# A branch for few tokens in the first half of the first layer, in three blocks of the last group

## The chip, the cores and the metric

One core of one Trainium2 chip. The metric is the device time of one execution in microseconds, as the median of several runs.

## What is computed

Linear attention with positive random features, then a layer of eight experts of which each token takes one. The attention output (4608 tokens of 512 values) is the experts' input; `e_idx` routes each token by the largest of its eight gate logits.

```python
for e in range(E):
    mask = e_idx == e
    h = np.maximum(x[mask] @ w1[e], 0.0)      # 512 -> 1024
    ye = h @ w2[e]                            # 1024 -> 512
    out[mask] = gate_w[mask, None] * eom[mask, e, None] * ye
```

## The kernel before, in words

The attention part works through 32 units and leaves its rows in DRAM. While it runs, tokens are routed in four groups; each group is cut into blocks of 128 tokens of one expert each. A block is one call of `item(n)` (line 1474 on). Blocks 0 to 24 belong to the first three groups. The last group holds blocks 25 to 48; in the part of the program that always runs (up to the first tail branch) these are blocks 25 to 37, thirteen of them. Blocks 25 to 35 are sure to hold tokens; 36 and 37 stand under a test of a flag (line 1491). With the data at hand the tail after them is not entered.

The work of a block on TensorE (PE) is cut in halves, which the text calls first half and second half of the first layer, and first and second half of the second layer:

- the first layer, `hidden(g, w_)` (line 1580), g = 0 and 1: 48 matmuls each (line 1588), a weight quarter of 128 x 128 as the stationary side and `w_` token columns as the moving side. Weights stand in fp16 as a high and a low part (`w1h`, `w1l`);
- `relu` on ScalarE (ACT, line 1595) and `rest` on VectorE (DVE, line 1599) make the high and low parts of the hidden values, `hh` and `hl`;
- the second layer, `second(g, w_)` (line 1604): 12 matmuls of 512 columns per half (line 1619), or 24 of 256 columns for few tokens (line 1611);
- `scaled` on ACT and `put` on GpSimd (POOL) write the rows out.

In the last group a block's second half of the first layer and its first half of the second layer are one step, "hB" (`hidden_and_second`, line 1626). The steps of neighbouring blocks alternate: the first half of block n's first layer ("hA"), the second half of block n-1's second layer ("out"), then block n's "hB".

A block with at most 64 tokens is one with few tokens. Its flag `few` is computed on the chip, loaded into a register of each engine (`load_flags`, line 1382), and tested by `either` (line 1567; the branch is line 1573 in the profile), which writes a step's code twice, for 64 and for 128 columns:

```python
with tc.If(regs[n, "few", (eng,)] > 0) as small_block:
    fn(FEW)
with small_block.Else():
    fn(P)
```

Before, in the last group all steps of a block but one go through `either`; the first half of the first layer does not and always takes 128 columns.

When the next block has another expert, its weights are brought in by SyncE (`bring`, lines 1507 and 1509; tiles `r`, `es`, `xs` and others), and cut into high and low parts by ACT (`high`, line 431) and DVE (`low`, line 435), a quarter at a time, as soon as the block before no longer needs that quarter. The last group has such changes of expert at blocks 26, 31 and 37.

The order of all steps is a table written out by hand (`ORDER`), and so are the PSUM banks; each engine's instructions stand in the program in that order. The code of all blocks is unrolled; there is no loop.

Of the kernel before, what the change touches and what calls it, by code (L numbers as in the profile page):

```python
# [21 lines left out]
P = 128  # L22
# [32 lines left out]
EARLIER = (8, 8, 9)  # L55
# [5 lines left out]
KS = (*EARLIER, NITEM - ISSUED[-1])  # L61
# [3 lines left out]
TAIL = (13, 18)  # L65
# [261 lines left out]
def attention_moe(ctx: ExitStack, tc: tile.TileContext, kqt, kqn, v, om, wg, w1, w2, cf, cm, ci, out):  # L327
# [1049 lines left out]
    slots = [(g, i) for g in range(NG) for i in range(KS[g])]  # L1377
    regs = {}
    EVERY = ("PE", "DVE", "ACT", "POOL", "SP")
    ENGINES = {"PE": ENG.PE, "DVE": ENG.DVE, "ACT": ENG.Activation, "POOL": ENG.Pool, "SP": ENG.SP}  # L1380

    def load_flags(n0, n1, row, engs):
        g, i = slots[n0]
        src = tabs[g]["few"][:, 0] if row == "few" else tabs[g]["ctl"][:, row]
        _, got = nc.values_load_multi_w_load_instructions(
            src[0:1, i : i + n1 - n0], engines=[ENGINES[e] for e in engs]
        )
        for m in range(n0, n1):
            regs[m, row, engs] = got[m - n0]
# [22 lines left out]
    def flags(g):  # L1412

        base = sum(KS[:g])
        R = -1000.0 + g
        sets = ("PE",), ("DVE",), ("ACT",), ("POOL",), ("SP",)
        cuts = sorted({base, base + KS[g], *(n for n in tail if base < n < base + KS[g])})

        def load(n0, n1, row, engs, part):
            after = [("limits" if row == "few" else "controls", g)] + ([("gi", g)] if g < NG - 1 else [])  # L1420
            if n0 >= 4:
                after.append(("out", n0 - 4, 1))
            plan.part = part
            plan.add(
                ("flag", n0, row, engs), engs, 0.5, lambda: load_flags(n0, n1, row, engs), after=after, rank=R,
            )
            plan.part = 0
            for m in range(n0, n1):
                flag_step[m, row, engs] = ("flag", n0, row, engs)

        rows = [(0, base + SURE[g], sets if g == NG - 1 else ()), (1, base, (("SP",), ("ACT", "DVE")) if g < FINE else (("SP",), ("ACT",), ("DVE",)))]
        if g == NG - 1 and FEW:
            rows.append(("few", base, (("PE",), ("ACT",), ("DVE",), ("POOL",))))
        for row, first, sets in rows:
            for a, b in zip(cuts, cuts[1:]):
                if row == 0 and a in tail:
                    load(a, a + 1, 0, EVERY, part_of(a) - 1)
                for n0 in range(max(a, first), b, BATCH):
                    for engs in sets:
                        load(n0, min(n0 + BATCH, b), row, engs, part_of(n0))  # L1440
# [8 lines left out]
    def cuts_of(n, w, parts=range(NQ)):  # L1449

        return [("sw", n, w)] if slots[n][0] < FINE else [("swl", n, w, i) for i in parts]
# [22 lines left out]
    def item(n):  # L1474
# [5 lines left out]
        def add(key, eng, cost, fn, after=(), **kw):  # L1480
            after = list(after)
            if not sure(n):
                after.append(flag_step[n, 0, (eng,)])
            if gr == NG - 1 and FEW and key[0] in ("hA", "hB", "relu", "rest", "out", "os", "put"):
                after.append(flag_step[n, "few", (eng,)])

            def step():
                if sure(n):
                    fn()
                else:  # L1490
                    with tc.If(regs[n, 0, (eng,)] > 0):  # L1491
                        fn()

            plan.add(key, (eng,), cost, step, after=after, **{"rank": R, **kw})
# [72 lines left out]
        def either(eng, fn):  # L1567

            if gr < NG - 1 or not FEW:
                return lambda: fn(P)  # L1570

            def step():
# [5 lines that stand above are left out]
            return step  # L1578

        def hidden(g, w_):  # L1580
            ph = banks["ph", n, g]
            for f4 in range(FC // 2):
                f = g * (FC // 2) + f4
                qd, fo = f // 2, (f % 2) * P
                a = 0
                for kk in range(KC):
                    for w, x in ((w1h, 2 * kk), (w1h, 2 * kk + 1), (w1l, 2 * kk)):
                        nc.tensor.matmul(  # L1588
                            ph[:, f4, 0:w_], w[qd][:, kk, fo : fo + P], xt(n)[:, x, 0:w_], start=(a == 0), stop=(a == 3 * KC - 1)
                        )  # L1590
                        a += 1

        def relu(g, w_):
            sl = slice(g * (FC // 2), (g + 1) * (FC // 2))
            nc.scalar.activation(hh(n)[:, sl, 0:w_], banks["ph", n, g][:, :, 0:w_], AF.Relu)  # L1595

        def rest(g, w_):
            sl = slice(g * (FC // 2), (g + 1) * (FC // 2))
            nc.vector.scalar_tensor_tensor(  # L1599
                out=hl(n)[:, sl, 0:w_], in0=banks["ph", n, g][:, :, 0:w_], scalar=0.0, in1=hh(n)[:, sl, 0:w_],  # L1600
                op0=ALU.max, op1=ALU.subtract,
            )
# [27 lines left out]
        for g in range(2):  # L1630
            name = "hA" if g == 0 else "hB"
            both = joint and g
            add(
                (name, n), "PE", 5.2 if both else 2.6,
                either("PE", hidden_and_second if both else lambda w_, g=g: hidden(g, w_)) if g else lambda: hidden(0, P),
                tiles=[("xt", n), ("hh", n), ("hl", n)] if both else [("xt", n)],
                bank=[("b", ("ph", n, g), [FC // 2, P])] + ([("b", ("po", n), [DM])] if both else []),
                after=[("xt", n), *cuts_of(n, 1, halves_of[g])]
                + ([("hA", n)] if g else [("hB", n - 1)] if joint and slots[n - 1][0] == gr else [])
                + ([("rest", n, 0), *cuts_of(n, 2, halves_of[0])] if both else []),  # L1640
                **(dict(early=2.6, lead={("rest", n, 0): 2.6, **{c: 2.6 for c in cuts_of(n, 2, halves_of[0])}}) if both else {}),
            )
            add(
                ("relu", n, g), "ACT", 0.48, either("ACT", lambda w_, g=g: relu(g, w_)), after=[(name, n)], rank=-600.0 + n,
                tiles=[("hh", n)],
            )
            add(
                ("rest", n, g), "DVE", 0.6, either("DVE", lambda w_, g=g: rest(g, w_)), after=[("relu", n, g)], rank=-600.0 + n,
                tiles=[("hh", n), ("hl", n)], frees=[("ph", n, g)],
            )  # L1650
# [43 lines left out]
    for n in range(len(slots)):  # L1694
        item(n)
# [80 lines left out]
```

## Time and profile before

| | |
|---|---|
| median of 3 runs | 621.66 us (620.2 to 622.68) |
| profiled execution, its own time | 623.94 us |
| its span, first to last instruction | 622.1 us |
| TensorE busy | 593.0 us, 95% |
| weight loads of TensorE busy | 470.7 us, 76% |
| VectorE, ScalarE, GpSimd busy | 388.7, 421.4, 373.9 us |
| mean DMA rate | 207 GB/s |

How to read it: a start is in us from the first instruction of the span. A busy time is the union of an engine's instructions, and matmuls overlap in it, so the spacing of their starts tells the rate and not their length. In a timeline row the bracket gives the time the engine stood still before the row and what the profile holds to have ended it; "issue" is a stop for which it shows no wait. "PEldq" is TensorE's sequencer, which reads the program ahead of the matmuls; branches stand there. "SPq" rows are transfers that SyncE issues. The queue "q8 instruction" moves TensorE's program code; its packets are told from the other engines' by their size.

### The profile page before, as it was taken

The page shows a single profiled execution, that of the slowest core. Times are in us where ns is not written, and L with a number is a line of the kernel's source. Part 1 is how long each engine was busy: PE and PEld are TensorE (multiplying, and loading weights), DVE is VectorE, ACT ScalarE, POOL GpSimd, SP SyncE. Part 2 cuts the span into 40 slices and gives each one's busy share as a digit, 9 for nine tenths or more (in the row PEclk, how much of TensorE's full clock was granted, in tenths as well). Part 3 has the DMA queues.
Part 4 walks back from the last instruction along what each step waited for, and adds up shares of the span by engine and source line. Part 5 has one row for each costly group of instructions (what it writes and reads, how often), then busy time and mean ns, then how long its engine had stood idle before and what let it go on. Part 6 is the DMA issues. An engine that isn't in the chain of part 4 may idle for free. (4 is left out here: it accounts for less than half of the span.)

```text
span 622.1 us, 22237 instructions
## 1 busy us (share of the span) xinstructions
PE 593.0 (95%) x8716; PEld 470.7 (76%) x8716; DVE 388.7 (62%) x1219; ACT 421.4 (68%) x978; POOL 373.9 (60%) x275
## 2 busy tenths in 40 slices
PE   6999986999999899999999999999999999999986
PEld 6999875877786677778877777777867867677764
DVE  4877699876688987657797855643783520361125
ACT  6999999789888688889968787872521521351134
POOL 1265589798977688999788789984413121211201
PEclk9999998899999999999999999999999999999999
DMA  7655689999999999999988999768677955842561
GB/s 255 210 167 164 204 286 198 227 224 272 312 259 232 238 255 206 285 199 239 303 217 246 237 204 191 180 168 228 200 155 225 222 102 180 241 79 55 162 224 45
DMA packets 145888, 129.00 MB, mean 207 GB/s; under 512 B 104270, under 2 KB 127440, under 8 KB 144464
## 3 DMA queue, kind: packets, MB, share of 16 engines
q1 hardware_dynamic: 139760, 107.45, 69.4%
q0 software_dynamic: 5984, 19.72, 10.5%
q8 instruction: 80, 1.31, 0.9%
q14 instruction: 64, 0.52, 0.3%
HBM read 83.86 MB, written 19.30 MB: 166 GB/s over the span
## 5 line engine op out<-in xcount | busy, mean ns | idle before, releaser
L1588 PE MATMUL ph<-xt,w1h 128*128 128x128 f16 (+1 forms) x2432 | 206.8, 218 | 3.7 <-issue 1.8
L1588 PE MATMUL ph<-xt,w1l 128*128 128x128 f16 (+1 forms) x1216 | 203.2, 218 | 0.0
L1588 PEld LDWEIGHTS <-w1h 128*128 128x128 f16 x2432 | 184.1, 98 | 12.1 <-issue 3.4
L625 ACT ACTIVATE ef<-pp,nb 128x128 f32<-128x128 f32 x576 | 163.2, 395 | 18.3 <-DVE nb L619 13.9
L606 DVE TENSOR_REDUCE pp<-pp 128x3 f32<-128x384 f32 x192 | 102.9, 558 | 32.8 <-PE pp L584 27.6
L648 POOL TENSOR_TENSOR es<-ef,es 128x1152 f16<-128x1152 f32 x44 | 104.5, 2386 | 25.6 <-ACT es L646 14.9
L1588 PEld LDWEIGHTS <-w1l 128*128 128x128 f16 x1216 | 118.5, 98 | 0.0
L1599 DVE SCALAR_TENSOR_TENSOR hl<-ph,hh 128x512 f16<-128x512 f32 (+1 forms) x76 | 50.5, 665 | 101.0 <-ACTq L1517 64.2
L1619 PE MATMUL po<-w2h,hl 128*128 128x512 f16 x280 | 106.1, 379 | 1.8 <-DVE hl L1599 1.8
L1619 PE MATMUL po<-w2h,hh 128*128 128x512 f16 x280 | 106.2, 379 | 0.2 <-PE ph L1588 0.2
L1619 PE MATMUL po<-w2l,hh 128*128 128x512 f16 x280 | 106.1, 379 | 0.0
L1595 ACT ACTIVATE hh<-ph 128x512 f16<-128x512 f32 (+1 forms) x76 | 44.6, 590 | 89.3 <-PE ph L1588 74.1
L1551 POOL DMA_INDIRECT gx<-rows,gi x38 | 38.8, 1020 | 89.0 <-ACT os L1674 34.7
L1619 PEld LDWEIGHTS <-hh 128*128 128x128 f16 x560 | 51.3, 98 | 52.7 <-issue 0.3
L518 POOL TENSOR_TENSOR xlo<-xt,xhi 128x1152 f16<-128x1152 f32 x24 | 57.1, 2379 | 9.3 <-ACT xhi L511 8.4
L1619 PEld LDWEIGHTS <-hl 128*128 128x128 f16 x280 | 27.4, 98 | 35.3 <-DVE hl L1599 2.3
L1674 ACT ACTIVATE os<-po,gx 128x512 f32<-128x512 f32 (+1 forms) x34 | 23.4, 687 | 43.1 <-PE po L1619 39.5
L646 ACT CAST es<-ef 128x1152 f16<-128x1152 f32 x44 | 51.5, 1181 | 0.7 <-ACTq L1512 0.2
L804 PE MATMUL pn<-kvs,et 128*128 128x81 f16 (+1 forms) x960 | 47.2, 203 | 0.9 <-DVE pp L606 0.5
L804 PEld LDWEIGHTS <-et 128*128 128x128 f16 (+1 forms) x960 | 40.3, 100 | 7.5 <-issue 0.5
L584 PE MATMUL pp<-omh,xhi 64*128 64x128 f16 x432 | 42.3, 222 | 2.7 <-DVE xf L817 0.8
L839 POOL TENSOR_TENSOR xs<-xf,xs 128x576 f16<-128x576 f32 x32 | 41.0, 1282 | 1.1
(193 smaller groups left out, 1057.7 us busy)
## 6 DMA issues: line engine op xcount, KB each, us to landing
r<-w SPq DMA_DIRECT2D x10, 2048.0 KB, 9.5
xt<-kqt SPq DMA_DIRECT2D x32, 576.0 KB, 5.1
xn<-kqn SPq DMA_DIRECT2D x24, 576.0 KB, 5.8
rawv<-v SPq DMA_DIRECT2D x32, 325.0 KB, 4.6
rows<-xs SPq DMA_DIRECT2D x16, 576.0 KB, 5.8
r<-w SPq DMA_DIRECT2D x8, 512.0 KB, 5.9
ef<-w SPq DMA_DIRECT2D x2, 512.0 KB, 4.3
et<-w SPq DMA_DIRECT2D x2, 512.0 KB, 8.1
```

The lines of the kernel that those rows point to most:

```text
L518: lambda t0=t0, t1=t1: nc.gpsimd.tensor_tensor(out=xl(u)[:, t0:t1], in0=xt32(u)[:, t0:t1], in1=xh(u)[:, t0:t1], op=ALU.subtract),
L584: nc.tensor.matmul(banks["pp", 2 * u + i, g][:, c, :], x[r, t], w[r, :], start=(a == 0), stop=(a == len(ops) - 1))
L606: nc.vector.tensor_reduce(out=pp[:, 3, 0:3], in_=pp[:, 0:3, :], op=ALU.min, axis=AX.X)
L625: nc.scalar.activation(ef(n)[:, c, :], banks["pp", n, g][:, c % 3, :], AF.Exp, bias=nb(n)[:, c : c + 1], scale=-SK)
L646: nc.scalar.copy(es(slot_es(n))[:, 0], ef(n))
L648: nc.gpsimd.tensor_tensor(out=es(slot_es(n))[:, 1], in0=ef(n), in1=es(slot_es(n))[:, 0], op=ALU.subtract)
L804: nc.tensor.matmul(pn[lo:hi, c - c0, :], a[:, c, lo:hi], w[:, :, b], start=(i == 0), stop=(i == len(ops) - 1))
L839: nc.gpsimd.tensor_tensor(out=x[:, :, P + o : P + o + D], in0=xf(u)[:, :, 0:D], in1=x[:, :, o : o + D], op=ALU.subtract)
L1588: nc.tensor.matmul(ph[:, f4, 0:w_], w[qd][:, kk, fo : fo + P], xt(n)[:, x, 0:w_], start=(a == 0), stop=(a == 3 * KC - 1))
L1595: nc.scalar.activation(hh(n)[:, sl, 0:w_], banks["ph", n, g][:, :, 0:w_], AF.Relu)
L1599: nc.vector.scalar_tensor_tensor(out=hl(n)[:, sl, 0:w_], in0=banks["ph", n, g][:, :, 0:w_], scalar=0.0, in1=hh(n)[:, sl, 0:w_], op0=ALU.ma ...
L1619: nc.tensor.matmul(po, x(n)[:, f, :], w[f // 2][:, f % 2, :], start=(f == 0 and a == 0), stop=(f == FC - 1 and a == 2))
```

## The change

`either` now also wraps the first half of the first layer, in blocks 25, 36 and 37. `tail_at` is 38, the last group has 24 slots, so `NARROW` is (25, 36, 37).

```diff
+    tail_at = sum(EARLIER) + TAIL[0]
+    NARROW = (len(slots) - KS[-1], tail_at - 2, tail_at - 1)
...
             add(
                 (name, n), "PE", 5.2 if both else 2.6,
-                either("PE", hidden_and_second if both else lambda w_, g=g: hidden(g, w_)) if g else lambda: hidden(0, P),
+                either("PE", hidden_and_second if both else lambda w_, g=g: hidden(g, w_)) if g or n in NARROW else lambda: hidden(0, P),
```

On TensorE, at the start of block 25's first half (`ph_25_0` is its PSUM tile, `xt25` its tokens, `po_24` the second layer of block 24), the program before has:

```order
L1619 LDWEIGHTS hl24_11711
L1619 MATMUL po_24_11772<-w2h1_100,hl24_11711 128x512
L1588 LDWEIGHTS w1h0_91
L1588 MATMUL ph_25_0_11785<-xt25_11749,w1h0_91 128x128
L1588 LDWEIGHTS w1h0_91
```

and now, at the start of the half and at the end of its first copy:

```order
L1622 MATMUL po_24_11772<-w2h1_100,hl24_11711 128x512
L1576 COMPARE_AND_BRANCH
L1591 LDWEIGHTS w1h0_91
L1591 MATMUL ph_25_0_11785<-xt25_11749,w1h0_91 128x64
...
L1591 MATMUL ph_25_0_11785<-xt25_11749,w1l1_96 128x64
L1576 UNCONDITIONAL_BRANCH
L1591 LDWEIGHTS w1h0_91
L1591 MATMUL ph_25_0_11785<-xt25_11749,w1h0_91 128x128
```

The half stands there twice: 48 weight loads and matmuls of 64 columns, a jump, and the 48 of 128 columns as before. Nothing changed places; the program after it stands 98 instructions further on.

The same at the start of block 36's first half on TensorE, now, behind the flag's own test:

```order
L1388 TENSOR_LOAD ctl3_11160
L1494 COMPARE_AND_BRANCH
L1576 COMPARE_AND_BRANCH
L1591 LDWEIGHTS w1h0_91
L1591 MATMUL ph_36_0_15283<-xt36_14953,w1h0_91 128x64
```

Before, the weight load of the 128-column half followed the first of the two branches. Block 37 is like block 36. The other engines' programs have the same instructions in the same order.

## Rows read from the trace of the kernel before

**Rows 1.** The core's span and clock; the page's queue of TensorE's code (packets, MB, share)
```profile
core 0: 622.1 us, clock 0.990
...
q8 instruction: 80, 1.31, 0.9%
```

**Rows 2.** Groups by line and shape, 64-column matmuls: count | busy us, mean ns | idle us
```profile
L1588 PE MATMUL ph<-xt,w1h 128*128 128x64 f16 x96 | 4.6, 193 | 0.0
L1588 PE MATMUL ph<-xt,w1l 128*128 128x64 f16 x48 | 4.5, 193 | 0.0
```

**Rows 3.** Timeline of TensorE, blocks 25 and 26: start us, length us, line, tiles, shape
```profile
482.69 0.27 PE L1588 MATMUL ph<-xt,w1h 128*128 128x128 f16 x2
...
485.37 0.38 PE L1619 MATMUL po<-w2h,hh 128*128 128x512 f16 x1
...
487.96 0.22 PE L1588 MATMUL ph<-xt,w1h 128*128 128x64 f16 x2
...
489.45 0.30 PE L1611 MATMUL po<-w2h,hh 128*64 128x256 f16 x2
...
498.57 0.38 PE L1619 MATMUL po<-w2h,hh 128*128 128x512 f16 x1
```

**Rows 4.** Timeline of TensorE: block 29's first and second half, block 36's second
```profile
522.24 0.28 PE L1588 MATMUL ph<-xt,w1h 128*128 128x128 f16 x2
...
527.51 0.27 PE L1588 MATMUL ph<-xt,w1h 128*128 128x128 f16 x2
...
603.63 0.22 PE L1588 MATMUL ph<-xt,w1h 128*128 128x64 f16 x2
```

**Rows 5.** Timeline of TensorE, the stops from block 25 to block 36
```profile
495.88 0.28 PE L1588 MATMUL ph<-xt,w1h 128*128 128x128 f16 x2 [0.71 <-ACT w2h L431]
...
530.55 0.38 PE L1619 MATMUL po<-w2h,hh 128*128 128x512 f16 x1 [0.20 <-PE ph L1588]
...
594.09 0.29 PE L1588 MATMUL ph<-xt,w1h 128*128 128x128 f16 x2 [1.82 <-issue]
```

**Rows 6.** Line 1573's branches on TensorE's sequencer: ns min/median/max, first and last start us
```profile
L1573 PEldq COMPARE_BRANCH  x1: 86/86/86, 485.1 to 485.1; - x1
...
L1573 PEldq COMPARE_BRANCH  x2: 190/941/1692, 493.8 to 494.1; - x2
...
L1573 PEldq COMPARE_BRANCH  x1: 330/330/330, 587.5 to 587.5; - x1
```

**Rows 7.** DMA queues, windows 493.3:591.8, 496.85:497.0, 535.43:535.6, 591.70:592.0, 598.33:598.5
```profile
q8 instruction: 17, 0.28, 1.2%
...
q8 instruction: 1, 0.02, 44.1%
...
q8 instruction: 1, 0.02, 40.5%
...
q8 instruction: 1, 0.02, 19.9%
...
q8 instruction: 1, 0.02, 42.4%
```

**Rows 8.** Timeline of SyncE: weight loads issued for blocks 26, 31, 37
```profile
483.72 1.77 SPq L1507 DMA_DIRECT2D es<-w  x2
...
522.29 7.89 SPq L1509 DMA_DIRECT2D r<-w  x2
...
586.50 0.36 SPq L1509 DMA_DIRECT2D r<-w  x1
...
592.06 0.36 SPq L1509 DMA_DIRECT2D r<-w  x1
```

**Rows 9.** Timelines of ScalarE, VectorE and TensorE, block 37's weights and last matmuls
```profile
606.70 2.00 ACT L431 ACTIVATE w1h<-r 128x1024 f16<-128x1024 f32 x2 [0.22 <-PE po L1611]
...
607.79 2.36 DVE L435 SCALAR_TENSOR_TENSOR w1l<-r,w1h 128x1024 f16<-128x1024 f32 x2 [0.85 <-ACT w1h L431]
...
616.02 0.30 PE L1611 MATMUL po<-w2l,hh 128*64 128x256 f16 x2 [0.74 <-DVE w2l L435]
```

## Prediction

> **What bounds the kernel.** From the page I took that TensorE is busy nearly all the time; the view of the core gives a mean granted clock of 0.990, so its speed is not in question [rows 1]. Then the groups by shape: first-layer matmuls of 64 columns come 96 and 48 times, three halves of 48 [rows 2]. The timeline shows what a half is worth by the spacing of its starts. Block 25, the last group's first, starts its first half at 482.69 and the next work at 485.37: 48 matmuls in 2.68 us, 0.0558 each. Its second half, with 64 columns, starts at 487.96 and the second layer at 489.45: 0.029 each and a short gap [rows 3]. A second such half starts at 603.63, in block 36 [rows 4]; the third is the last half of all, in block 37. So the three blocks that get a branch are the three that can use it.
>
> Next the idle time of TensorE from block 25 on. It stands still three times before the last block: 0.71 us before 495.88, 0.20 before 530.55, 1.82 before 594.09 [rows 5]. The last falls inside 48 like matmuls and is put down to "issue": the next instruction was not there. The first is put down to a weight cut of ScalarE, but TensorE's own branch into that half, at 494.1, took 1.692 us, to 495.8 [rows 6]; I take it for the same thing. Another branch, at 587.5, took 0.330 [rows 6].
>
> The DMA view has a queue of kind "instruction", 80 packets of 16 KB [rows 1]. From the first of these stops to the last it has 17 [rows 7], and in the built program 16 x 256 instructions lie between the two places. So TensorE's code comes in pieces of 256 instructions, and I can say where their edges are. I count from block 25's first weight load (a matmul is two, a branch one, a branch to the next row none): the last stop comes at position 4673, the others fit, and the edges are at 65 + 256k.
>
> When does a piece come? The edge at 4417 is passed by the branch at 587.5, so at 587.9; the next packet starts at 591.7, and the stop at its end, 594.09, shows that code is usable 2.4 us after its packet starts [rows 5 to 7]. A weight load issued at 586.50 was under way [rows 8]. Likewise 594.1 to 598.33, with the load of 592.06, and 530.6 to 535.43, with the second load of the row at 522.29: 3.8 to 4.8 us from edge to packet [rows 5, 7, 8]. In a quieter stretch it was 1.1, from 495.8 to 496.9 [rows 6, 7]. So a piece needs about 3.4 us in quiet and 6.2 to 7.2 under a load, and only one is asked for ahead. The branch at 485.1 ran when some 42 of 48 matmuls had started: TensorE's queue is read about 36 instructions ahead [rows 3, 6].
>
> **The change, part by part.** Nothing is removed and no step is moved. Each of the three first halves gets a branch, a 64-column copy of 96 instructions and a jump over the old one: 98 more in the program each. The order of steps is a fixed table, so no other engine's work moves.
>
> (a) The matmuls: 48 x (0.0558 - 0.029) = 1.27 us less in each of three blocks, 3.8 in all. The branch costs nothing: it is read while the queue holds second-layer matmuls, as at 485.1, where it took 0.086 us [rows 6]. Without that cover it would be its 0.09, and 0.33 for the jump.
>
> (b) Block 37's share comes to nothing. From 607.79 VectorE splits weights and residues with hardly a gap, and the last second-layer matmuls wait 0.74 for it at 616.02 [rows 9]. That chain starts with ScalarE's cut at 606.70, behind block 36's second half [rows 9], not behind block 37's first. A shorter first half makes TensorE wait longer. Bounds: 0 to 0.7 us won.
>
> (c) Block 25. More code is passed in less time. The edge at 321 is passed at 487.6, in the load issued from 483.72 [rows 8]. With 4.0 us to the packet and 2.4 to its use the piece is there at 494.0. TensorE needs it at position 577, now five matmuls before the end of block 26's first half, at 492.0. It waits 2.0, does 0.3 and 1.4 us more, and starts block 26's second half at 495.7 (before: 495.88). The edge at 833 comes 15 matmuls in; that piece takes 3.3 from 494.0, so 0.8 more is waited. The half ends at 499.1 against 498.57 [rows 3]: 0.5 us lost in place of 1.27 won. Bounds: -2.0 (the 1.27 and the old 0.71, no new wait) to +1.4 (4.8 us to the packet).
>
> (d) Blocks 29 and 30. Their code is the same, 98 places later. The edge at 1857 now lies inside block 29's first half, which starts at 522.24 [rows 4]; it is passed at 522.9, just after the load issued at 522.29 [rows 8]. The edge at 2113 is now the first instruction of block 29's second half, needed at 527.51 [rows 4]; before, it lay past that half and cost the 0.20 at 530.55. With 4.0 + 2.4 the piece is there at 529.3: 1.8 waited. TensorE jumps the edge at 2369 at about 537.1; the piece behind it takes 6.4, to 543.5, and TensorE is at 2625, inside block 30's second half, at 542.4: 1.1 more. Less the 0.2, +2.7 us. Bounds: 0 (the request slips in ahead of the load) to +3.4 (4.8 us).
>
> (e) Blocks 35 and 36, in the times of before. The edge at 4673 is now jumped by the branch into block 35's second half, its piece asked for before the load of 586.50: the stop of 1.82 goes, 2.0 by the matmuls' spacing. Block 36's first half is 1.27 shorter. But the edge at 4929 now lies in it, passed at 596.9 in the load of 592.06, and the edge at 5185 comes 26 matmuls into its second half, 4.3 us later; the piece takes 6.4. New wait 2.1, sum -1.2. Bounds: -3.3 (no new wait) to -0.4 (4.8 us).
>
> (f) In block 37 a piece comes every 3.3 us and TensorE will stop again for a microsecond or two in all; the chain of (b) covers it, and without that cover it would be paid.
>
> Sum: 0.5 + 2.7 - 1.2 = **+2.0 us**. The profiled execution has a span of 622.1 [rows 1] and a time of 623.94; the median of the runs is 621.66. So 624.1 by the span, **623.6** by the median. A measurement of this kernel can tell 0.5%, 3.1 us, from no change: I forecast no change that can be told, to the slow side.
>
> The rows show code waited for while a load is under way [rows 5, 7, 8]. The Trainium skill, page "Runtime: NRT & Kernel Launch", section "Instruction fetch mechanics", says that code streams in 16 KiB blocks of 256 instructions, that crossing an edge is "mostly hidden", and that a taken branch out of the two blocks held stalls. The trace agrees on the block and the branch; it differs on "mostly hidden" inside loads. By that phrase the sum would be (a) without (b), -2.5 us.
>
> **Rivals.** First, the code comes in time: blocks 25 and 36 give 1.27 each, block 37 nothing. For it: only three stops in 110 us. Against it: the same pieces are used up faster, and each edge named above falls into a load. It gives 621.66 - 2.5 = 619.1, and 616.4 if the old stops of (c) and (e) go as well.
>
> Second, slower: every request in a load waits as long as that of 530.6, 4.8 us. Place: edges 321, 1857 and 4929. For it: this is the only request that met the first packets of a load, as 1857's will. Price: 1.4 + 3.4 - 0.4 = 4.4, so 626.1; it passes 3.1 from about 4.4 us on.
>
> Third: the flags choose the full copy and nothing is saved. The 64-column rows, chosen by the same flag, speak against it [rows 2]. The code still moves, so (d) would stay: 624.4.
>
> **How the numbers follow.** Forecast, 0.62: 623.6, own range 620.5 to 625.5, a tenth of it over 624.8. First rival, 0.21, something over half of it under 618.5, where the old stops go too. Second, 0.15, and third, 0.02, over 624.8 for the most part. So faster 0.13, same 0.64, slower 0.23. One case in ten is left out at each end: 618.4, inside the first rival, to 626.1, the second's price.
>
> **What would show it.** In the changed profile the 64-column matmuls double, from 144 to 288. TensorE stops near 492 inside block 26's first half, near 528 before block 29's second, near 542 inside block 30's second and near 604 inside block 36's second; it does not stop inside block 35's second half. Each stop ends about 2.4 us after an instruction packet starts. The last second-layer matmuls still wait for VectorE. I am wrong if TensorE runs through blocks 26 and 29 without a stop (first rival), if a stop there is over 2.5 us (second), or if the end no longer hangs on VectorE.

## The result, and the profile after

The changed kernel takes 625.84 us (median of 16 runs, 622.99 to 631.2), the kernel before, in turn with it on the same chip, 622.17 (16 runs, 619.99 to 628.45). The ratio is 1.0064, with a 95% interval of 1.0042 to 1.0086: **slower by 4.0 us**, 2.6 to 5.4. I had forecast 2.0 more and no change that can be told. The time fell inside my range (to 626.1), at its upper end.

The profiled execution has a span of 622.8 us, hardly more than before [rows 1], but block 25 begins at 480.23 in it and began at 482.69 before. What lies ahead of block 25 differs from run to run by several us (480 to 492 in the seventeen traces of this case), in kernels that are alike there. So the two traces are compared from the start of block 25 to the start of the last matmul: 133.80 us before (482.69 to 616.49), **136.88** after (480.23 to 617.11), 3.1 more. The last matmul is the second of the two in these rows, before and after:

```profile
616.46 0.30 PE L1611 MATMUL po<-w2h,hl 128*64 128x256 f16 x2
```

```profile
617.08 0.30 PE L1614 MATMUL po<-w2h,hl 128*64 128x256 f16 x2
```

The page's queue of TensorE's code, and the groups by line and shape:

```profile
q8 instruction: 81, 1.33, 0.9%
```

```profile
L1591 PE MATMUL ph<-xt,w1h 128*128 128x64 f16 x192 | 9.4, 193 | 2.7 <-issue 2.4 <-PE po L1614 0.3
L1591 PE MATMUL ph<-xt,w1l 128*128 128x64 f16 x96 | 9.2, 193 | 0.0
```

The 64-column matmuls have doubled, from 144 [rows 2] to 288, and those of line 1591 (1588 before) now stand idle for "issue". The timeline of TensorE, blocks 25 and 26, to hold against [rows 3, 5]:

```profile
480.23 0.22 PE L1591 MATMUL ph<-xt,w1h 128*128 128x64 f16 x2
...
481.63 0.38 PE L1622 MATMUL po<-w2h,hh 128*128 128x512 f16 x1
...
487.14 0.28 PE L1591 MATMUL ph<-xt,w1h 128*128 128x128 f16 x2
...
492.70 0.28 PE L1591 MATMUL ph<-xt,w1h 128*128 128x128 f16 x2 [2.87 <-issue]
...
496.79 0.26 PE L1591 MATMUL ph<-xt,w1l 128*128 128x128 f16 x1 [0.46 <-issue]
...
499.00 0.38 PE L1622 MATMUL po<-w2h,hh 128*128 128x512 f16 x1
```

Block 25's first half takes 1.40 us, 481.63 less 480.23, in place of 2.68. Three matmuls before the end of block 26's first half TensorE stops for 2.87. The same stretch in windows (the columns are busy us and count of PE, PEld, DVE, ACT, POOL, then granted clock, DMA share, GB/s):

```profile
489.80:492.70 2.90, 0.03 (x2) 0.01 (x1) 2.33 (x3) 0.79 (x1) 0.00 (x0) 1.00 1.42 261
492.70:494.07 1.37, 1.37 (x23) 1.27 (x25) 0.00 (x0) 0.94 (x2) 0.00 (x0) 1.00 0.52 115
494.07:497.48 3.41, 2.95 (x29) 2.40 (x26) 2.78 (x3) 1.55 (x2) 0.00 (x0) 0.50 0.73 82
497.48:499.00 1.52, 1.52 (x30) 1.52 (x28) 0.18 (x1) 0.00 (x0) 0.00 (x0) 1.00 0.04 11
```

From 494.07, 1.37 us after the stop ended, TensorE's granted clock is 0.50 for 3.41 us, the 1.2 GHz level: 29 matmuls start in that time, where the 1.52 us behind it hold 30. No row of the kernel before had shown this in this stretch. It does not cost what it slows down, because a second stop for code, 0.46 before 496.79, lies inside these 3.41 us: what TensorE did slowly ahead of 496.79 it would else have spent waiting for that piece. The comparison with e6 below puts the price of the low clock at 0.6 us at most.

The later stops, from the same timeline:

```profile
528.30 0.29 PE L1591 MATMUL ph<-xt,w1h 128*128 128x128 f16 x2 [0.19 <-PE po L1622]
...
541.76 0.23 PE L1591 MATMUL ph<-xt,w1h 128*128 128x128 f16 x1 [0.68 <-issue]
...
604.32 0.23 PE L1591 MATMUL ph<-xt,w1h 128*128 128x64 f16 x2 [1.67 <-issue]
...
608.62 0.30 PE L1614 MATMUL po<-w2l,hh 128*64 128x256 f16 x2 [0.67 <-issue]
...
611.98 0.22 PE L1591 MATMUL ph<-xt,w1h 128*128 128x64 f16 x2 [0.68 <-issue]
...
616.64 0.30 PE L1614 MATMUL po<-w2l,hh 128*64 128x256 f16 x2 [0.34 <-DVE w2l L435]
```

The first three are where the forecast put them: ahead of block 29's second half, inside block 30's and block 36's second halves. Those at 608.62 and 611.98 belong to block 36's second layer and block 37, part (f). The stop of 1.82 inside block 35's second half [rows 5] is gone. By stretch, counted from block 25's start:

| up to | before | after | difference in the stretch | forecast |
|---|---|---|---|---|
| end of block 26's second half | 15.88 | 18.77 | (c) +2.89 | +0.5 |
| start of block 31 | 63.57 | 67.34 | (d) +0.88 | +2.7 |
| end of block 36's second half | 122.44 | 124.81 | (e) -1.40 | -1.2 |
| start of the last matmul | 133.80 | 136.88 | (f) +0.71 | 0 |

### The profile page after: what moved, and what is told of

Its sections match the earlier page's. It is cut to its first block, busy times and chain, and to the rows that moved or that the text cites. A ratio compares the mean times of both kernels' runs of the same rounds, so it can differ in the third digit from the quotient of the medians.

```text
span 622.8 us, 22241 instructions
## 1 busy us (share of the span) xinstructions
PE 588.7 (95%) x8716; PEld 466.4 (75%) x8716; DVE 388.6 (62%) x1219; ACT 421.2 (68%) x978; POOL 374.1 (60%) x275
## 5 line engine op out<-in xcount | busy, mean ns | idle before, releaser
L1591 PE MATMUL ph<-xt,w1h 128*128 128x128 f16 (+1 forms) x2432 | 204.7, 218 | 6.6 <-issue 5.9
L1591 PE MATMUL ph<-xt,w1l 128*128 128x128 f16 (+1 forms) x1216 | 200.7, 217 | 0.5 <-issue 0.5
L1591 PEld LDWEIGHTS <-w1h 128*128 128x128 f16 x2432 | 181.8, 98 | 16.4 <-issue 9.3
```

Source lines behind the costliest of these rows:

```text
L1591: nc.tensor.matmul(ph[:, f4, 0:w_], w[qd][:, kk, fo : fo + P], xt(n)[:, x, 0:w_], start=(a == 0), stop=(a == 3 * KC - 1))
```

## The experiments

The theory: TensorE's code comes in pieces, an edge that is passed while a weight load is under way waits for it, and the 98 new instructions in a block move all later edges. The rivals: the branches cost a time of their own; the narrow halves bring nothing; the loss has to do with something else than code. Ratios are against the kernel before, run in turn on the same chip; the groups e1 to e4, e5 to e8, e9 to e12 and e13 to e15 ran on four different chips, on which the kernel before takes 630.6, 630.8, 623.6 and 631.5 us. "Length" is that from block 25's start to the last matmul's start, in the one profiled execution.

| run | ratio, 95% interval | length, us |
|---|---|---|
| changed kernel | 1.0064, 1.0042 to 1.0086 | 136.88 |
| e1, block 25 alone | 1.0010, 0.9982 to 1.0039 | 140.16 |
| e2, blocks 36 and 37 | 0.9991, 0.9962 to 1.0019 | 135.81 |
| e3, gain without code | 0.9949, 0.9917 to 0.9980 | 133.03 |
| e4, code without gain | 1.0019, 0.9992 to 1.0045 | 136.69 |
| e5, kernel before again | 1.0009, 0.9975 to 1.0043 | 136.10 |
| e6, changed kernel again | 1.0031, 1.0001 to 1.0060 | 135.47 |
| e7, no copies | 0.9902, 0.9869 to 0.9935 | 128.52 |
| e8, half loads | 0.9969, 0.9938 to 1.0000 | 132.16 |
| e9, 96 idle instructions | 0.9945, 0.9914 to 0.9975 | 132.04 |
| e10, all thirteen blocks | 1.0129, 1.0085 to 1.0174 | 139.84 |
| e11, copies in three blocks | 0.9990, 0.9963 to 1.0017 | 130.21 |
| e12, the same without the change | 0.9952, 0.9917 to 0.9987 | 130.68 |
| e13, no load for block 26 | 0.9990, 0.9953 to 1.0028 | 132.12 |
| e14, e2 and 48 idle instructions | 0.9961, 0.9928 to 0.9994 | 133.65 |
| e15, e9 again | 0.9982, 0.9956 to 1.0009 | 133.91 |

### Parts of the change: e1 to e4

e1 and e2 take a part of the tuple:

```diff
-    NARROW = (len(slots) - KS[-1], tail_at - 2, tail_at - 1)
+    NARROW = (len(slots) - KS[-1],)              # e1
+    NARROW = (tail_at - 2, tail_at - 1)          # e2
```

> Only block 25 gets the branch and the narrow copy; blocks 36 and 37 are as before. Theory (TensorE's code comes late): block 25's 98 new instructions alone move every later edge, so the stops of 2.9 us in block 26's first half and the small ones in blocks 29 and 30 stay, the old stop of 1.8 us inside block 35's second half goes, and nothing is saved in block 36: +2.9 to the end of block 26's second half, +0.9 more to block 31, -1.9 at block 35, together +2.0 us against the kernel before (ratio about 1.003). Rival (each branch and its jump cost about 1 us where they stand): a third of the whole loss of 3.7 us, +1.2, with 64-column halves followed by a gap at the branch itself and no stop in block 26. Rival (something ahead of block 25 differs): nothing later than block 25 changes in length.

> Blocks 36 and 37 get the branch and the narrow copy; block 25 is as before. Theory (code late): up to block 35 the trace is that of the kernel before (stops of 0.7 in block 26, 0.2 in block 29, 1.8 in block 35). In block 36 1.27 us are saved, and a new stop of about 0.9 comes behind its first half, where the edge that the new code brings is passed in the second weight load: -0.3 us, which is the same time; block 37's share is covered by VectorE's splits. Rival (each branch costs about 1 us): +2.5 us. Rival (code in time, the forecast's first): -1.3 us.

e3 has the narrow halves without branch or second copy, e4 the branch and two copies of 128 columns:

```diff
-either("PE", ... lambda w_, g=g: hidden(g, w_)) if g or n in NARROW else lambda: hidden(0, P)
+... if g else (lambda: hidden(0, FEW)) if n in NARROW else lambda: hidden(0, P)             # e3
+either("PE", ... lambda w_, g=g: hidden(g, w_ if g else P)) if g or n in NARROW else ...    # e4
```

> The first halves of blocks 25, 36 and 37 are done with 64 columns always, without a branch and without the copy of 128 columns (left out: the tokens past 64 that such a block could hold with other data). The matmuls are those of the changed kernel, and the code lies where it lay before the change. Theory (code late): 1.27 saved in block 25, of which the stop in block 26 gives some back (0.7 becomes about 1.6, since the same piece is asked for and wanted earlier); -0.7 to block 35, whose stop of 1.8 stays; -1.27 in block 36, block 37's covered: -2.0 us (bounds -1.3 and -2.6). Rival (the narrow first halves themselves bring nothing, since others wait): 0 or more, and with the changed kernel's loss in them about +3.7.

> The changed kernel with 128 columns in both copies of the three first halves: the same 98 instructions in each place, nothing saved. Theory (code late): stops in blocks 25 and 26, 29, 30 and 36 as in the changed kernel, a little shorter where TensorE now arrives 1.27 us later: about +4 us against the kernel before, within 1 us of the changed kernel, because what is saved there is spent waiting for code. Rival (the loss comes of the 64-column form, the code costs nothing): 0 us. Rival (the change's saving of 2.5 us is real and paid in full): the changed kernel's +3.7 and 2.5 more, +6.2.

e3 decides the first point: the narrow halves alone win 3.2 us (1.3 to 5.2 by the interval). So the matmuls that the change saves are worth what they seemed (the 2.0 expected lies inside the interval), and the new code costs more than they give. The stop of 1.6 that I expected in e3's block 26 did not come; the 1.81 in block 35 stayed. e4, the code alone, comes out at +1.2 us (-0.5 to +2.8): less than the 4 expected, which lies outside the interval; 0, the first rival's value, lies inside. Its trace has the "issue" stops of block 26's second half (1.43), block 30 (0.23) and block 36 (0.45), shorter than the changed kernel's. e1 and e2 are both the kernel before's time within their intervals; they do not tell the parts apart. In e1's trace the stop is in block 26's second half, 4.46 us long, and the clock falls behind it as in the changed kernel:

```profile
504.98:508.39 3.41, 3.41 (x30) 2.86 (x28) 0.02 (x1) 0.60 (x1) 0.00 (x0) 0.50 0.42 75
```

e1's length is the longest of all and its time is not, so single traces of block 26 differ more than I had thought.

### The two kernels again, all copies gone, and lighter loads: e5 to e8

e5 and e6 are the two kernels unchanged.

> The kernel before once more, for a trace from the chip of the runs beside it. Theory (code late): the stops that hang on the place of the code come again at the same instructions, at the 18th matmul of block 35's second half (1.7 to 2.1 us) and ahead of block 29's second-layer work (0.2 to 0.5); their length may differ by a microsecond, since it hangs on when the weight load begins. If the 1.85 us that the runs without a change in blocks 36 and 37 also waited in block 36's second-layer work, behind ScalarE, come here too, they belong to the chip and not to an edit. Rival: the stops move about from run to run.

> The changed kernel once more, beside the kernel before on the same chip. Theory (code late): stops at the same instructions as before: in block 26 at the 45th matmul of the first half or the 14th of the second, 1.6 to 4.6 us together; ahead of block 29's second half; at the 37th matmul of block 30's second half; at the 27th of block 36's second half. From block 25's start to the last matmul it is 2 to 4 us longer than the kernel before, and the ratio of the times lies between 1.003 and 1.007. Rival (the loss comes from another part of the program): the distance from block 25's start to the last matmul is the same in both.

The stops came at the same instructions. In e5 TensorE stands 1.84 us behind the 18th matmul of block 35's second half, and 0.75 ahead of block 29's second layer (0.2 to 0.5 expected); in e6 there are stops behind the 45th matmul of block 26's first half and the 14th of its second, ahead of block 29's second half, behind the 37th matmul of block 30's second half and the 27th of block 36's, as in the first trace. But block 26's are 0.52 and 1.16 here, and no clock falls behind them:

```profile
500.86 0.29 PE L1591 MATMUL ph<-xt,w1h 128*128 128x128 f16 x2 [0.52 <-issue]
...
504.68 0.22 PE L1591 MATMUL ph<-xt,w1l 128*128 128x128 f16 x1 [1.16 <-issue]
...
506.57 0.38 PE L1622 MATMUL po<-w2h,hh 128*128 128x512 f16 x1
```

From the first stop's end to the second's, and from there to the end of the half, in windows, first e6, then the changed kernel's first trace:

```profile
500.86:504.68 3.82, 2.66 (x42) 2.24 (x42) 3.14 (x6) 2.49 (x3) 0.00 (x0) 1.00 0.53 77
504.68:506.57 1.89, 1.89 (x34) 1.89 (x34) 1.15 (x2) 0.00 (x0) 0.00 (x0) 1.00 0.04 9
```

```profile
492.70:496.79 4.09, 3.63 (x41) 2.98 (x42) 2.09 (x3) 2.49 (x3) 0.00 (x0) 0.67 0.75 103
496.79:499.00 2.21, 2.21 (x34) 2.21 (x34) 0.87 (x1) 0.00 (x0) 0.00 (x0) 0.84 0.09 14
```

Ahead of the second stop TensorE is busy 3.63 us for the same work that takes it 2.66 in e6, and yet this stretch is only 0.27 longer: the piece comes when it comes. Behind it the low clock costs 0.32 more. So by this comparison at most 0.6 of the two stretches' 6.30 us are the clock's.

Block 26's load starts at another moment against the code, first in the changed kernel's first trace, then in e6:

```profile
481.25 1.97 SPq L1510 DMA_DIRECT2D es<-w  x2
```

```profile
487.24 0.93 SPq L1510 DMA_DIRECT2D es<-w  x2
```

That is 1.0 us behind block 25's start at 480.23, and 2.8 us ahead of block 25's start at 490.04. In e6 another request met it, the one behind the edge at 65: its packet comes 3.9 us behind block 25's start (493.98), where it came 1.6 behind it in the first trace (481.82). From block 25's start to the end of block 26's second half e6 takes 16.53 us and e5 15.69, +0.84 where the first pair of traces has +2.89. Why the load starts at different times is not shown.

The ratio on this chip is 1.0031: the sign stands, the size is half. By the lengths alone e6 would not be slower than e5 (135.47 against 136.10), where I had expected 2 to 4 us more and named equal lengths as the rival's sign. TensorE's waits from block 25 on say why, for e5:

```profile
PE ph L1588 <- issue: 1.8, 1, 1.8
PE po L1611 <- ACT hh L1595: 1.6, 1, 1.6
...
PE po L1611 <- DVE w2l L435: 0.7, 1, 0.7
...
```

The wait of 1.6 for ScalarE in block 36 is not in the first trace of the kernel before; I come back to it at the end.

e7 takes the branch and the copy that does not run out of TensorE's blocks 25 to 37:

```diff
         def either(eng, fn):
+            if eng == "PE" and gr == NG - 1 and n < tail_at:
+                return lambda: fn(FEW if n in NARROW else P)
```

> TensorE's blocks 25 to 37 hold one copy each, 64 columns in blocks 25, 36 and 37 (both halves and the second layer) and 128 in the others, without branch or jump; left out is the choice by the flag, so only this data's blocks come out. The matmuls that run are those of the changed kernel; some 2500 instructions that do not run are gone. Theory (code late): no stop for code is left, since TensorE then takes 7 us for 256 instructions; the three stops of the kernel before (2.7) and the narrow halves (2.5, block 37's covered) are won, -4 to -6 us against the kernel before (ratio 0.990 to 0.994), -7 to -9 against the changed kernel. Rival (code costs nothing, the narrow halves are worth 2.5): -2.5 us. Rival (neither counts): 0.

-0.98%, some 6.2 us under the kernel before and, by the ratios, 8 under the changed kernel, whose matmuls it runs: inside the expected ratio. Its queue of code and its waits from block 25 on:

```profile
q8 instruction: 70, 1.15, 0.8%
```

```profile
PE po L1617 <- DVE hl L1605: 0.5, 1, 0.5
PE po L1617 <- ACT hh L1601: 0.4, 1, 0.4
PE po L1617 <- DVE w2l L435: 0.4, 1, 0.4
```

No stop for "issue" is left. This falls with the theory alone: the rivals expected -2.5 or 0.

e8 halves the loads for blocks 31 and 37 (half of each expert's weights is left out):

```diff
-                nc.sync.dma_start(r1 if which == 1 else r2, (w1 if which == 1 else w2)[bass.ds(r, P)])
+                t, w = (r1, w1) if which == 1 else (r2, w2)
...
+                    nc.sync.dma_start(t[:, 0 : t.shape[1] // 2], w[bass.ds(r, P), 0 : t.shape[1] // 2])
```

> The changed kernel with half of each of the four weight loads for blocks 31 and 37 (half of the rows of the expert's weights stay the last expert's: left out). Program and code as in the changed kernel; block 26's load is whole. Theory (TensorE's code waits behind these loads): the stop in block 26 stays; those ahead of block 29's second half, in block 30's second half and in block 36's second half shrink from 2.5 us together (in the trace of the changed kernel) to under 1; packets come 1 to 2 us after their edge in place of 3 to 5: -1.5 to -2.5 us against the changed kernel, so +1 to +2.5 against the kernel before. Rival (code comes late by itself, whatever else is under way): the same stops, +3 to +4.

-0.31% against the kernel before and, by the ratios, 3.9 us under e6: more than expected. TensorE's waits from block 29's stretch to the end (530 us on), first e6, then e8:

```profile
PE ph L1591 <- issue: 3.0, 3, 1.5
PE ph L1591 <- ACT os L1677: 0.8, 1, 0.8
...
```

```profile
PE po L1618 <- ACT hh L1602: 1.6, 1, 1.6
PE po L1618 <- DVE w2l L435: 0.7, 1, 0.7
PE ph L1595 <- issue: 0.6, 1, 0.6
...
```

The 0.8 that the view gives to ScalarE is the stop ahead of block 29's second half. Program and code are those of e6; the "issue" stops go from 3.0 to 0.6 with the bytes of the loads. The code waits behind the loads. Not all of the gain is that: half a load is also ready earlier for the cuts. And 1.6 of what the stops give comes back in this trace as block 36's wait for ScalarE.

### The place and the amount of code: e9 to e12

e9 is the kernel before with one more call in a copy that this data never runs:

```diff
             hidden(1, w_)
+            if n == 34 and w_ < P:
+                hidden(1, w_)
             second(0, w_)
```

> The kernel before with 96 instructions that never run with this data: block 34's 64-column copy does its first-layer half twice, and block 34 holds over 64 tokens. Not one executed instruction is added or taken away. Theory (what counts is which instruction the edge of a piece falls on): the edge that lies inside block 35's second half moves out of it and is asked for ahead of the weight load; the stop of 1.7 to 2.0 us at the 18th matmul there goes, no other place changes, and from block 25's start to the last matmul it is 2 us shorter than in the kernel before: ratio about 0.997. Rival (the stop belongs to the weight load or to this half's data): same stop, same time. Rival (more code is slower whatever its place): a little over 1.

-0.55%, 3.4 us (1.6 to 5.4): more than the 2 expected, with 2 inside the interval. The timeline has block 35's second half and the start of block 36 with no stop between:

```profile
588.75 0.28 PE L1588 MATMUL ph<-xt,w1h 128*128 128x128 f16 x2
...
594.02 0.28 PE L1588 MATMUL ph<-xt,w1h 128*128 128x128 f16 x2
```

48 matmuls of 0.0558 and 12 of 0.216 are 5.27 us, and 594.02 - 588.75 is 5.27; in the kernel before the same stretch had the 1.82 [rows 5] in it. 96 instructions that are never run, all of them in the block before, took the stop away: it hangs on where the edge falls and on nothing that is computed.

e10 gives all thirteen blocks the branch:

```diff
+    NARROW = range(len(slots) - KS[-1], tail_at)
```

> The change in all thirteen blocks: ten more first halves get a branch and a 64-column copy that they never take (98 instructions each). Theory (code late): ten times a branch over 96 instructions that are fetched and not run, so TensorE comes to each edge earlier and stops more; by the place of the edges +2 to +4.5 us against the kernel before, so about as much as or up to 2 us more than the changed kernel, with stops of 3 us or more in block 26 and of 1 to 2 in blocks 29, 30 and 36. Rival (each branch costs a fixed time of 0.1 to 0.3 us): +1 to +3 us over the changed kernel, spread evenly over the ten blocks with no stop at an edge. Rival (code costs nothing): -2.5.

+1.29%, 8 us (5.3 to 10.9): above what I expected. That would leave room for the rival, a fixed time for each branch, but the trace does not: from block 31's start to that of block 35's second half, where e10 has no stop, it takes 44.85 us (554.12 to 598.97) with the branches and the kernel before 44.84 (546.26 to 591.10) without. The stop in block 26 is 5.06 us, and the clock is down for 3.41 us twice, behind it and in block 36. The timeline and the windows:

```profile
496.30 0.39 PE L1591 MATMUL ph<-xt,w1h 128*128 128x128 f16 x2 [5.06 <-issue]
...
611.68 0.19 PE L1591 MATMUL ph<-xt,w1l 128*128 128x64 f16 x1 [1.76 <-issue]
```

```profile
495.94:499.35 3.41, 3.05 (x29) 3.05 (x30) 0.71 (x1) 0.00 (x0) 0.00 (x0) 0.50 0.55 103
611.99:615.40 3.41, 3.41 (x36) 2.96 (x34) 0.87 (x2) 1.91 (x3) 0.00 (x0) 0.50 0.22 82
```

e11 and e12 keep copies, in all engines, only where blocks hold few tokens; e12 leaves the first halves as they were before:

```diff
-            if gr < NG - 1 or not FEW:
+            if gr < NG - 1 or not FEW or (n < tail_at and n not in NARROW):
                 return lambda: fn(P)
...
-if g or n in NARROW else lambda: hidden(0, P),
+if g else lambda: hidden(0, P),                                          # e12 alone
```

> Copies in TensorE's and the other engines' programs only in blocks 25, 36 and 37, all parts of them, the first halves too as in the change; the other ten blocks always take 128 columns, which they do with this data anyway (right for any data). Some 1900 instructions that never run are gone. Theory (code late): the stops in blocks 29, 30 and 35 go; a stop of 1 to 3 us stays in block 26, where block 25's two copies lie against the load, and one of about 0.6 in block 36: -3 to -5 us against the kernel before (ratio 0.992 to 0.995). Rival (the change loses by itself, whatever the code around it): the time of e12 or above. Rival (code costs nothing): -2.5.

> As e11, but without the change: first halves of all blocks at 128 columns, copies of the other parts only in blocks 25, 36 and 37. Theory (code late): against the kernel before the stops in blocks 29 and 35 go and that in block 26 shrinks to about 0.5: -2.5 to -3 us (ratio 0.995 to 0.996). Against e11: e11 has 2.5 us less of matmuls and 1 to 2 us more of stops, so it should be 0 to 2 us faster than this one, where the change on the full set of copies lost 2 to 4. Rival (code costs nothing): the time of the kernel before.

e12 is at -0.48%, as expected, and its waits from block 25 to the end are one row:

```profile
PE po L1614 <- DVE w2l L435: 0.8, 1, 0.8
```

e11 missed: -0.1%, where -0.5 to -0.8% was expected. Its length, 130.21, is in the span that was expected, and its trace has the stop in block 26 as named:

```profile
PE ph L1591 <- issue: 1.8, 2, 1.5
```

So in this trace e11 is 0.5 us under e12, and in the times it is not (0.9990 against 0.9952, the intervals overlap). e11's trace also has a wait of 1.28 us for the DMA of block 25's tokens, just ahead of where the length begins. I can't say what its other executions do; that the stop in block 26 is often longer than 1.5 there would fit, and is not shown.

### Block 26's load, and a better place: e13 to e15

What had failed in the forecast was block 26. e13 takes its load and cuts away:

```diff
         def bring(which):
+            if n == ALT:
+                return
...
         def cut(which, i, eng):
+            if n == ALT:
+                return
```

> The changed kernel without the weight load and the cuts for block 26 (left out: block 26 and those behind it until 31 use the last expert's weights). TensorE's program is the same but for one wait. Theory (the step that was mis-sized: TensorE's code waits behind block 26's load): packets behind block 25's edges come 1 to 2 us after the edge in place of 3.6 to 5.4; the stops in block 26, 2.8 to 3.9 us in the changed kernel's two traces, come down to 0 to 1.7 us; those in blocks 29, 30 and 36 stay: -2 to -3.5 us against the changed kernel, from 1 us above to 2 us below the kernel before. Rival (in blocks 25 and 26 the code is simply used up faster than it can come, load or no load): stops of 2.8 us or more in block 26, and the changed kernel's time.

The timeline of TensorE in e13 has no stop in block 26; those in blocks 29, 30 and 36 stay (0.83, 0.56 and 1.29), as expected:

```profile
491.56 0.29 PE L1595 MATMUL ph<-xt,w1h 128*128 128x128 f16 x2
...
495.84 0.29 PE L1595 MATMUL ph<-xt,w1h 128*128 128x128 f16 x2
...
498.80 0.38 PE L1626 MATMUL po<-w2h,hh 128*128 128x512 f16 x1
```

From the start of block 26's first half to the start of its second layer it takes 7.24 us (498.80 - 491.56); the changed kernel takes 11.86 (499.00 - 487.14). The piece behind the edge at 321 comes at 491.13, 1.6 us after the edge (some 4.9 us into block 25); in the changed kernel it comes at 490.50 to 490.60, 5.4 after it. The packet in the DMA view of the changed kernel, in that window of 0.1 us:

```profile
q8 instruction: 1, 0.02, 60.0%
```

So it is block 26's own load, with its cuts, that holds the code back; without it the narrow half does not use the code up too fast. In time e13 is at -0.10% (-0.47 to +0.28): where the change loses 2 to 4 us, this loses nothing that can be told.

e14 and e15 try the place of the code for a gain. e14 is e2 with half of e9's pad, e15 is e9:

```diff
+            if n == 34 and w_ < P:
+                hidden(1, w_, FC // 4)                                   # e14: two of the four groups
```

> Blocks 36 and 37 get the branch and the narrow copy, block 25 does not (as e2), and block 34's 64-column copy, which does not run with this data, does half of its first-layer half twice (48 instructions more that never run). Theory (the edge's place): as in e9 the stop inside block 35's second half goes (2.0), and 1.27 are saved in block 36, with 1 to 1.6 us of new stops behind block 36 of which VectorE's splits cover most: -2.5 to -3.5 us against the kernel before, with e9's time or up to 1.3 us under it. Rival (e9's gain was the chip's noise): -1.3 or more.

> The kernel of e9 once more, beside e13 and e14: again no stop inside block 35's second half, and a ratio to the kernel before of 0.994 to 0.998. Rival (noise): 1.0 and a stop.

e14: -0.39%, 2.5 us (0.4 to 4.5), under the kernel before; its rival, -1.3 or more, is inside that interval. e15: -0.18% (-0.44 to +0.09), just outside the ratio of 0.994 to 0.998 that was expected; the stop in block 35 is gone again. Three kernels that are written to be right for any data lie under the kernel before with their whole interval: e9 (but not in its second group, e15), e12 and e14. Which of them is best isn't settled.

## Why the prediction was right and wrong

**The mechanism** was right: each of the stops that was named came, within two matmuls of the place named for it, the one in block 35 went, and the end still waits for VectorE. e7, e9 and e13 show what the forecast only argued: take away the code that is not run, move an edge, or take away the load, and the stops go.

**(a)** 1.27 us in a half: right, 1.28 in block 25, and e3 shows that they are worth their time where the code does not move. The branches cost nothing that a row shows (e10).

**(c)** is the step that failed: "It waits 2.0 ... so 0.8 more is waited", +0.5 us in all. It was +2.89. The term that was mis-sized is the time of a piece of code beside block 26's load. The request behind the edge at 321 took 5.4 us, not 4.0, and lay outside my upper bound of 4.8, which I had from the loads of blocks 31 and 37 alone; the stop ended 12.47 us after block 25's start, not 11.31, 1.2 later. The piece behind the edge at 833 came 4.09 us after that, not 3.3: 0.8 more. The rest of the half took 2.21 us for 1.8, for the granted clock was still 0.50 up to 497.48. Together these are the 2.4 us that were missing. The clock I had not priced at all ("its speed is not in question [rows 1]"), and a mean of 0.990 over the span does not tell what a new stop does to it; but by the comparison with e6 it is at most 0.6 of the 2.4. In e6 (c) is +0.84 against e5, near the forecast: there the load began 3.8 us earlier against block 25 and held another request. When the load begins against the code is not a term of the forecast, and one number for (c) could not be right for both executions.

**(d)** was too high: +0.88 for +2.7. The edge at 1857 was passed at 523.3 by the matmuls' spacing, and its packet came at 525.88, 2.6 us later, not 4.0; the stop behind it was 0.36 by the matmuls' spacing in place of 1.8. In block 30 it was 0.68 by the profile for 1.1.

**(e)** was right: -1.40 for -1.2. The 1.82 went, 1.67 came in block 36 for the 2.1 forecast.

**(b) and (f)** were right in the cover, and wrong in its width. VectorE's timeline of block 37, after a row of the kernel before:

```profile
614.07 0.42 DVE L1599 SCALAR_TENSOR_TENSOR hl<-ph,hh 128x256 f16<-128x256 f32 x1
```

```profile
612.84 1.23 DVE L435 SCALAR_TENSOR_TENSOR w2l<-r,w2h 128x1024 f16<-128x1024 f32 x1 [0.17 <-ACT w2h L431]
614.59 0.42 DVE L1602 SCALAR_TENSOR_TENSOR hl<-ph,hh 128x256 f16<-128x256 f32 x1 [0.53 <-ACT hh L1598]
615.36 1.23 DVE L435 SCALAR_TENSOR_TENSOR w2l<-r,w2h 128x1024 f16<-128x1024 f32 x1 [0.35 <-DVE hl L1602]
```

The chain that covers TensorE has block 37's own remainder in it, ahead of the last split. Before, VectorE came to it without a wait; now TensorE's stops at 608.62, 609.38 and 611.98 (0.67, 0.35 and 0.68) outweigh the 1.27 saved, VectorE waits 0.53 for it, and the split is late with it: 0.71 at the end. What I called a cover waits for what it was to cover.

So the sum came to +3.1 in this trace in place of +2.0, with an error of +2.4 and one of -1.8 in it that nearly cancelled: that it came so near is luck. The times say 4.0 on this chip and some 2 on e6's. The first rival (code in time) is dead by both traces of the changed kernel; so is the third, by the 288 matmuls. The second, "a stop there is over 2.5 us", was nearest: its mark was met by block 26, but not by all loads, since blocks 29 and 30 waited less; that its 626.1 lies nearest to the time is no proof of it.

The Trainium skill, page "Runtime: NRT & Kernel Launch", section "Instruction fetch mechanics", calls the crossing of an edge "mostly hidden". e7, in which every edge behind block 25 is crossed without a stop, and block 26 of e13 bear that out; the stops of 1.67 and 2.87 us in the changed kernel speak against it where a load is under way.

## What to carry to other kernels

In unrolled code with copies for two cases, count the instructions that are not run: they come by DMA too, and near a weight load an edge that moves can cost more than the matmuls that a copy saves. Before adding a copy, ask which edges it moves, which load each of them meets, and whether that load always begins at the same moment; leaving out a copy that this data never runs (e12), or adding a pad (e9), can be worth more than the shorter half. Where the clock falls between two stops for code, price it by what the second stop would else have been. A single trace is not enough for a step that hangs on when a load begins. A cover at the end is to be followed instruction by instruction, for steps in it that wait for the covered engine.

## What the runs showed of the hardware that was not expected

TensorE's clock: after stops of 2.87 us (changed kernel), 4.46 (e1), and 5.06 and 1.76 (e10) the granted clock was 0.50 for 3.41 us each time, from 1.37 and 0.57 us behind the stop's end in the first two, from 0.36 ahead of it in the third and 0.31 behind it in the last. After 1.82 in the kernel before, 1.84 in e5 and 1.67 in the changed kernel's block 36 it stayed at 1.00. In e2, e4, e6, e7 and e14 it was 0.50 for 3.41 us once ahead of block 25, beside several stops of 0.2 to 1.2 us each; in e1, e3, e5, e8, e13 and e15 it stayed at 1.00 beside stops of that size there. So the length of one stop alone does not decide it; no run here takes this apart.

The 1.6 us in block 36: in e1, e2, e3, e5, e8 and e15 ScalarE's activation of block 36's second half starts 1.65 to 1.71 us after GpSimd issues the store just ahead of it, and TensorE waits 1.6 us for it; in the first trace of the kernel before, in e9, e11 and e12 store and activation start together, with the same instructions. In e6 the activation starts 1.67 us after the store too, but TensorE's stop of 1.51 us comes ahead of it, and nothing is left to wait for; that can be a reason why the change loses less on the chip of e5 and e6. It is not the chip alone: e7, from the same one, has 0.13. What causes it I did not find.
